# Talking-heads attention and squared-ReLU feed-forward: fifteen fused tiles instead of twenty in the first batch, and a third score block of 64 queries

## The chip, the cores and the metric

The kernel runs on one core of one Trainium2 chip. The metric is the device time of one execution in microseconds (us); lower is better.

The core has a matrix engine (TensorE; PE in the profile, PEld for its weight loads), a vector engine (DVE), a scalar engine (ACT), a general engine (POOL) that here also issues the loads from HBM, and SyncE (SP), whose queue issues the copies between on-chip tensors ("gathers") and the stores of the output. Matrix products land in PSUM, which this program uses as eight banks; operands lie in SBUF.

## The reference

Eight batches, twelve heads, 448 queries and keys, head size 64. What is computed, cut to what matters:

```python
scores = np.matmul(q, k.transpose(0, 1, 3, 2)) / np.sqrt(64)
scores = np.einsum('bhij,hg->bgij', scores, w_pre)      # mix the 12 heads
attn = softmax(scores, axis=-1)
attn = np.einsum('bhij,hg->bgij', attn, w_post)         # mix them again
x = np.matmul(attn, v)                                  # then (b, s, h*d): 3584 rows of 768
h = np.maximum(x @ w_in, 0.0)                           # 768 -> 2048
out = (h * h) @ w_out                                   # 2048 -> 768
```

## The kernel before

**Tiles and steps.** A batch's 448 queries are cut into 45 tiles of ten (the last has eight). A tile holds 12 heads x 10 queries = 120 rows of 448 scores, so that mixing the heads is one matmul with a fixed 120x120 matrix. The program is one list of steps, one tile per step, eight batches one after the other. Step `i` does the head mixing and the exponential of tile `i` (`mix`), and four steps later (`LAG`) the second mixing (`unmix`), whose result DVE copies out of PSUM (L461). Between these, attention-times-V units (`av_unit`), transposes of the next batch's q and k (`turn_unit`) and feed-forward units (`ffn1_unit`, `ffn2_unit`) are put in at fixed steps or as "filler", spread over the steps by weights. Each engine runs its instructions in program order; nothing is chosen at run time.

**Two ways to mix.** In the usual way, `score_burst` computes the scores of a block of 128 queries for six heads at a time (L365; L371 where the block is the short one of 64 queries, in which two heads share a matmul's columns). ACT and DVE copy them from PSUM into a tile `S` (L375, L377). `S` has two buffers, used in turn: a block can be written only when all gathers that read the block two before it have landed. Then `gather` copies the rows of one tile from `S` into a tile `G` of 120 rows with a DMA on SP's queue (L394; where the tile lies in the short block, two DMAs of half the heads, L397; where it lies across the border to it, three), and `mix` is one matmul (L426). `G` has twelve buffers. In the first batch the first `FUSED` tiles are made without scores and gathers: DVE multiplies q by the mixing weights ahead of time (`mix_queries`, L196), and `mix` is six matmuls straight from k and those products (L412).

**Order.** `ORDER` lists the tiles of the first batch by step. In it, gathered tiles stand between fused ones in pairs. `gathered` is the list of all gathered tiles in that order. From step 2 on, each step may issue up to two gathers, up to ten (at the start twelve) ahead of the gathered tiles mixed so far (`AHEAD`). A burst hangs on a gather: `BURSTS[b][blk]` names the gathers of block `blk`, counted from the block's first tile (`FIRST`), behind which the next block's bursts stand in the program. `STARTS` gives each block's first query. `EARLY` says from which steps the first batch's feed-forward units, in thirds of the queries, become filler: (step, third, from, to).

**Loads.** POOL issues the loads of w_in (L266, `W1_AT`), w_out (L272, `W2_AT`), v (L249, L253) and the next batches' q and k (L88, `KQ_AT`) at fixed steps. SP's DMAs go round eight completion semaphores, and the ninth in a row waits for the first to land.

## Time and profile before

| | |
|---|---|
| time, median of 3 runs | 591.75 us (590.99 to 591.92) |
| the profiled execution | 590.49 us, its span 588.7 us |
| granted TensorE clock | 0.999 |
| busy share | PE 96%, PEld 62%, DVE 68%, ACT 65%, POOL 60% |
| DMA | 72.28 MB, mean 123 GB/s |
| HBM | read 47.28 MB, written 11.01 MB |
| SP's queue (gathers and stores) | 36.1% of 16 engines' span |
| POOL's queue (loads) | 30.8% of 16 engines' span |

The busy share of PE is that of modelled matmul ends, which overlap the next matmul's start; start to start tells more than the duration of one. All times of the trace are counted from the span's start. "Idle before <-X" names what ended the idle time of an engine.

### The profile page before, as it was taken

Reading aid. Unit: us, or ns where it says so; the run is one execution under the profiler, and the core shown is the slowest. Engines: PE = TensorE matmul, PEld = TensorE weight load, DVE = VectorE, ACT = ScalarE, POOL = GpSimd, SP = SyncE. Lnnn points to the kernel's source line nnn. Section 1 sums busy time; section 2 is a strip of 40 time slices with the busy share of each in tenths; the row PEclk is TensorE's granted clock in tenths of the full one; section 3 lists DMA queues with packets and bytes.
Section 4 is the critical chain, followed back from the end, with each engine's and each line's share of the span. In section 5 each row is a group of like instructions: output and inputs, shape, how many; then the busy total and the mean of one; then the engine's idle time right before and its main releaser. Section 6 shows DMA issues by size and latency. Waiting matters only on the chain.

```text
span 588.7 us, 18500 instructions
## 1 busy us (share of the span) xinstructions
PE 566.1 (96%) x6735; PEld 363.0 (62%) x6735; DVE 401.1 (68%) x995; ACT 380.3 (65%) x1114; POOL 355.2 (60%) x812
## 2 busy tenths in 40 slices
PE   3999999998999999999999999999999999999996
PEld 2577767665566565666665665665565666666554
DVE  7766759777777667866877578867777667755011
ACT  3756878576886558775876558775677648862410
POOL 6576895465677338783578437783387436772730
PEclk9999999999999999999999999999999999999999
DMA  9999999599568754697558955687544865432113
GB/s 128 146 192 188 182 199 179 109 140 193 118 116 144 162 120 90 115 152 150 109 97 132 166 119 100 118 148 149 107 75 70 131 135 106 87 49 55 28 27 82
DMA packets 85579, 72.28 MB, mean 123 GB/s; under 512 B 18768, under 2 KB 80496, under 8 KB 85488
## 3 DMA queue, kind: packets, MB, share of 16 engines
q1 hardware_dynamic: 49354, 47.30, 36.1%
q0 software_dynamic: 35552, 23.60, 30.8%
q8 instruction: 53, 0.87, 0.6%
q14 instruction: 38, 0.31, 0.2%
q10 hardware_dynamic: 582, 0.21, 0.2%
HBM read 47.28 MB, written 11.01 MB: 99 GB/s over the span
## 4 chain that ended last, share of the span: by engine, by line
PE 82%; DMA 9%; ACT 4%; DVE 2%; POOL 1%; issue 1%; SPq 0%; ACTq 0%; POOLq 0%
PE o_ps L323 24%; PE h_ps L279 23%; PE m_ps L426 10%; PE at_ps L455 9%; DMA G<-S 7%; PE ot_ps L228 5%; PE s_ps L365 4%; ACT S L375 2%; ACT e L430 2%; PE m_ps L412 2%; PE tr_ps L213 2%; PE ot_ps L235 2%; PE at_ps L459 1%; DMA kst<-in_k_dram 1%; PE s_ps L371 1%
## 5 line engine op out<-in xcount | busy, mean ns | idle before, releaser
L430 ACT ACTIVATE e<-m_ps 120x448 bf16<-120x448 f32 x360 | 196.2, 551 | 85.2 <-PE m_ps L426 47.5
L461 DVE CAST at<-at_ps 128x480 bf16<-128x480 f32 (+1 forms) x360 | 206.4, 591 | 62.9 <-PE at_ps L459 46.8
L440 POOL TENSOR_SCALAR pn<-post,rc 120x120 bf16<-120x120 bf16 (+1 forms) x340 | 122.6, 371 | 169.1 <-DVE rc L437 101.8
L279 PE MATMUL h_ps<-xt,w 128*128 128x448 bf16 (+2 forms) x960 | 169.3, 315 | 0.4 <-DVE at L461 0.2
L323 PE MATMUL o_ps<-w,h 128*128 128x384 bf16 x768 | 138.7, 326 | 0.4 <-ACT e L430 0.2
L426 PE MATMUL m_ps<-G,pre 120*120 120x448 bf16 (+1 forms) x340 | 121.3, 357 | 3.5 <-ACT S L375 1.4
L279 PEld LDWEIGHTS <-w 128*128 128x128 bf16 x960 | 84.0, 97 | 56.9 <-issue 6.9
L455 PE MATMUL at_ps<-pn,e 120*128 120x120 bf16 x1080 | 115.9, 216 | 3.1 <-ACT S L375 2.1
L290 POOL TENSOR_TENSOR h<-hr 128x384 bf16<-128x384 f32 (+1 forms) x144 | 105.7, 736 | 21.6 <-ACT hr L285 19.9
L455 PEld LDWEIGHTS <-e 120*128 120x128 bf16 x1080 | 85.5, 98 | 49.3 <-ACT S L375 5.4
L285 ACT ACTIVATE hr<-h_ps 128x448 f32<-128x448 f32 (+2 forms) x160 | 76.2, 480 | 50.0 <-PE h_ps L279 37.0
L323 PEld LDWEIGHTS <-h 128*128 128x128 bf16 x768 | 73.1, 98 | 47.9 <-issue 4.7
L375 ACT CAST S<-s_ps 128x448 bf16<-128x448 f32 x177 | 82.4, 552 | 13.7 <-PE s_ps L365 10.2
L377 DVE CAST S<-s_ps 128x448 bf16<-128x448 f32 x141 | 79.7, 612 | 2.8 <-DMA G<-S 2.4
L430 ACT ACTIVATION_READ_ACCUMULATOR e<-m_ps 120x1 f32 x360 | 75.7, 210 | 0.0
L332 DVE COPY osb<-o_ps 128x384 f32<-128x384 f32 x54 | 30.0, 556 | 57.0 <-PE o_ps L323 56.8
L437 DVE RECIPROCAL rc<-sm 120x2 f32<-120x2 f32 (+1 forms) x192 | 31.1, 162 | 47.9 <-ACT e L430 34.2
L426 PEld LDWEIGHTS <-pre 120*120 120x120 bf16 (+1 forms) x340 | 44.9, 132 | 19.0 <-issue 10.8
L443 POOL TENSOR_TENSOR en<-e,rc 120x128 bf16<-120x128 bf16 (+1 forms) x112 | 42.5, 380 | 0.0
L241 ACT CAST xt<-ot_ps 128x450 bf16<-128x450 f32 (+1 forms) x48 | 25.4, 532 | 25.7 <-PE ot_ps L235 25.2
L365 PE MATMUL s_ps<-kT,qT 64*128 64x448 bf16 x276 | 40.5, 357 | 1.6 <-ACT e L430 0.7
L228 PE MATMUL ot_ps<-at,v 128*64 128x150 bf16 x864 | 41.5, 229 | 0.0
(62 smaller groups left out, 473.4 us busy)
## 6 DMA issues: line engine op xcount, KB each, us to landing
G<-S SPq DMA_DIRECT2D x276, 105.0 KB
out_dram<-osb SPq DMA_DIRECT2D x54, 192.0 KB
kst<-in_k_dram POOLq DMA_DIRECT2D x14, 336.0 KB, 6.3
qst<-in_q_dram POOLq DMA_DIRECT2D x14, 336.0 KB, 6.1
G<-S SPq DMA_DIRECT2D x70, 52.5 KB
v<-in_v_dram POOLq DMA_DIRECT2D x8, 384.0 KB, 8.1
w<-in_moe_w_in_dram POOLq DMA_DIRECT2D x6, 512.0 KB, 11.0
w<-in_moe_w_out_dram POOLq DMA_DIRECT2D x8, 384.0 KB, 8.0
```

The costliest lines, as they stand in the source:

```text
L228: nc.tensor.matmul(ps[64 * hh:64 * hh + 64, TQ * y:TQ * y + TQ], lhsT=vts[b % 2][:, g, r, :], rhs=at[:, r, g, :, :].rearrange("p t i -> p ...
L279: nc.tensor.matmul(ps[:, 0:n], lhsT=w1[ft // 8][:, c2, ft % 8 * 128:ft % 8 * 128 + 128], rhs=xts[b][:, c2, n0:n1], start=(c2 == 0), stop=( ...
L285: nc.scalar.activation(out=hr[:, 0:n], in_=ps[:, 0:n], func=ACT.Relu)
L290: eng.tensor_tensor(out=dst[:, x - o:y - o], in0=hr[:, x - n0:y - n0], in1=hr[:, x - n0:y - n0], op=ALU.mult)
L323: nc.tensor.matmul(ps[:, 0:384], lhsT=lhsT, rhs=w2[ft // 4][:, ft % 4, nt * 384:(nt + 1) * 384], start=(ft == 0), stop=(ft == FT - 1))
L375: nc.scalar.copy(out=sb[:, h, :], in_=ps[:, 0:S])
L377: nc.vector.tensor_copy(out=sb[:, h, :], in_=ps[:, 0:S])
L426: nc.tensor.matmul(ps[0:n, 0:S], lhsT=m[0:n, 0:n], rhs=Gs.pop(s)[0:n, :], start=True, stop=True)
L430: nc.scalar.activation(out=e[0:n, x, :], in_=ps[0:n, 0:S], func=ACT.Exp, scale=SCALE, accum_out=sm[0:n, x:x + 1])
L440: nc.gpsimd.tensor_scalar(out=esb[(b, t - z)][1][0:rows, :], in0=(post_gi if fused else post)[0:rows, :], scalar1=rc[0:rows, z:z + 1], sca ...
L455: nc.tensor.matmul(ps[:, RG * r:RG * r + RG], lhsT=e[0:n, tl % 2, P * r:P * r + P], rhs=pn[0:n, :], start=True, stop=True)
L461: nc.vector.tensor_copy(out=ats[(b, third)][:, 0:k, :, tl, :], in_=ps[:, 0:k * RG].rearrange("p (r g i) -> p r g i", r=k, i=IQ))
```

## The change

In the first batch only fifteen tiles (0 to 14) are fused; tiles 15 to 44 are gathered. The order of the steps is new: after the seven fused tiles at the start comes one gathered tile, then fused and gathered tiles take turns in pairs up to step 21, and from step 22 on all tiles are gathered, in order. The scores of the first batch are cut into three blocks that start at queries 150, 256 and 384, in place of two that start at 200 and 320; the last has 64 queries, as in the other batches. So block 0 serves tiles 15 to 25, block 1 tiles 26 to 38, block 2 the rest of tile 38 and tiles 39 to 44. The bursts hang on other gathers: those of block 1 on the tiles at 4 and 8 of block 0, that of block 2 on tile 6 of block 1 (tile 32), those of the next batch's block 0 on tiles 2 and 4 of block 2 (tiles 41 and 43; before, tiles 40 and 43). The filler of the first thirds of the feed-forward begins at steps 29, 34 and 39 (before 26, 32, 38).

```diff
-FUSED = 20
+FUSED = 15
-ORDER = [0, *range(1, 7), 20, 21, *range(7, 11), 22, 23, *range(11, 15), 24, 25, 15, 16, 17, 26, 27, 18, 19, *range(28, 45)]
+ORDER = [*range(7), 15, 7, 8, 16, 17, 9, 10, 18, 19, 11, 12, 20, 21, 13, 14, *range(22, 45)]
-STARTS = {0: (FQ, S - 128)}
-FIRST = {0: (FUSED, 32)}
-BURSTS = {0: ([4, 8], [8, 11])}
+STARTS = {0: (FQ, 256, 384)}
+FIRST = {0: (FUSED, 26, 39)}
+BURSTS = {0: ([4, 8], [6], [2, 4])}
-EARLY = ((26, 0, 0, 2), (32, 0, 2, 4), (38, 1, 0, 4), (52, 2, 0, 4))
+EARLY = ((29, 0, 0, 2), (34, 0, 2, 4), (39, 1, 0, 4), (52, 2, 0, 4))
```

In `score_burst` and `gather` the short block is known by its start (a query past 320) and no longer by its number 3. In `mix` the first batch takes its mixing matrix as the others do, so that the tiles of the short block get the one with the halved order of heads:

```diff
+        short = q0 > S - P
-                if blk < 3:
+                if not short:
-            for c in range(2 if blk == 3 else 0):
+            for c in range(2 if short else 0):
...
-            if blk < 3:
+            if STARTS[b][blk] <= S - P:
...
-            m = pres[max(x for x in pres if x <= t)] if b else pre
+            m = pres[max(x for x in pres if x <= t)]
```

## The prediction

> **What bounds the kernel now.** I read the chain of waits first, in order of time, over the whole span:

> ```profile
> 14.43 2.51 PE m_ps L412 x6
> 17.60 1.28 PE m_ps L412 x6
> ...
> 23.53 10.45 DMA G<-S
> 34.64 1.14 PE m_ps L412 x6
> ...
> 41.02 14.22 DMA G<-S
> ```

> Columns: start, length, what. A warm fused tile costs PE 1.14 us, six matmuls of 0.19. From 34 us on PE follows itself, one fused tile behind another, and PE is busy 9.95 of 10 us between 30 and 40 us (busy time by stretches), while DVE has 5.5. The start of the program is PE's. But two gathers stand in the chain: the fourth, issued at 23.53, lands at 33.98; the eighteenth, issued at 41.02, lands at 55.24, after 14 us. So fourteen gathers land in 21.26 us, **1.52 us each**, however early they are issued. The DMA view of 40 to 66 us tells why:

> ```profile
> q0 software_dynamic: 2877, 3.23, 79.6%
> q1 hardware_dynamic: 1878, 1.55, 21.9%
> ```

> POOL's loads and SP's gathers fill all sixteen engines (79.6 + 21.9). Between 23 and 60 us the gathers come as fast as the loads let them.

> Third, the timeline of batch 1's end, where one burst's eviction meets a late gather:

> ```profile
> 131.67 0.99 PE L365 MATMUL s_ps<-kT,qT 64*128 64x448 bf16 x6
> ...
> 132.59 0.40 PE L426 MATMUL m_ps<-G,pre 120*120 120x448 bf16 x1
> ...
> 134.47 1.84 ACT L375 CAST S<-s_ps 128x448 bf16<-128x448 f32 x4 [2.21 <-DMA G<-S]
> 134.53 1.16 DVE L377 CAST S<-s_ps 128x448 bf16<-128x448 f32 x2 [2.02 <-DMA G<-S]
> 135.05 0.17 PEld L455 LDWEIGHTS <-e 120*128 120x128 bf16 x3 [2.34 <-ACT S L375]
> 135.05 0.33 PE L455 MATMUL at_ps<-pn,e 120*128 120x120 bf16 x3 [2.07 <-ACT S L375]
> ```

> The block for these scores takes the `S` buffer that tile 44's gather still reads. That gather lands at 134.21 (completion counts of SP's queue). Until then ACT and DVE stand, in order, with everything behind them; PE does one more mixing, has six of eight banks full of scores, and stops until 135.05, **0.84 us after the landing**. In the first batch of before this wait costs nothing: the next batch's burst (step 30) takes the buffer of tiles 20 to 31, the first twelve gathers, landed by 43.2.

> **The change, part by part.**

> *Fused tiles.* Five times six L412 matmuls become five L426: 5 x (1.14 - 0.19) = 4.7 us less on PE, all before step 28, where PE bounds. DVE loses five eighths of six L196 operations (0.65 us each, about 2.1 us, not on the path at 5.5 to 6.6 of 10).

> *Third block.* Twelve L371 matmuls on quarters of the array and six evictions, four on ACT (0.55) and two on DVE (0.61), at step 22. Its buffer is that of the first eleven gathers, the last of which landed at 41.7 in before; step 22 falls at about 42. Should ACT hold PE up there, the time comes out of the stall of step 31, below, so I put it at nothing; without that cover it is ACT's 2.2 us.

> *Pairs.* The third gather (landed 32.20) is wanted at step 11, about 30.6, and PE waits 1.6 us; the others up to step 21 are there. Five gathers more, and eight more DMAs, since tile 38 takes three and 39 to 44 two each: 0.77 us each on SP, and the eight semaphores now hold about four tiles. SP has idle time; it costs only if the gathers become the bound.

> *They do, at the burst of (1, block 0).* It hangs on tile 41, gather 27 of the new list. That is issued in the program when seventeen gathered tiles are mixed, which is step 31. The blocks now take buffers 0, 1, 0, 1, so this burst waits for block 1's readers, tiles 26 to 38: the first DMA of tile 38 is the 24th gather. Behind the waiting evictions stand, on ACT, the exponentials from step 32 and the ReLUs, on DVE the L461 copies and reciprocals, and behind these PE's banks, POOL, and the w_out loads from step 32 on.

> When does the 24th land? At 1.52 us each from the eighteenth: 55.24 + 6 x 1.52 = 64.4. Before's own 24th (tile 43) landed at 64.57 by the completion counts, next in line as soon as the one before it was through, so an earlier issue gains little. Nearer bound: v's small packets pass between 55 and 59 us and gathers 19 to 22 landed 0.8 us apart there (57.10 to 59.53); if SP's earlier issue and the w_out loads held back by the stall stretch that, 62.3. I take 64.4, the rate of the whole stretch. PE reaches the burst at 53 to 54 (4.7 us less work, 1.6 us waited, then the sixteenth and seventeenth gathers at 50.4 and 52.8), so all of the gain is waited away. PE goes on at 64.4 + 0.84 = 65.2, after the mixing of step 32. In before that place is here (PE's timeline):

> ```profile
> 59.31 0.35 PE L426 MATMUL m_ps<-G,pre 120*120 120x448 bf16 x1
> 59.50 0.32 PE L455 MATMUL at_ps<-pn,e 120*128 120x120 bf16 x3
> ```

> 65.2 - 59.5 = **5.7 us later**.

> *EARLY.* Before, eight feed-forward units of six L279 matmuls (0.39 us) were done by then. After, they begin behind step 29, whose transposes are charged against them: about three by step 32. Five are left for the steps behind the stall, where PE stands little (0.3 us between 60 and 67): 5 x 0.39 = **1.95 us**. The floor is nothing, if they fill waits for ACT between 67 and 82, where PE, start to start, stood 2.5 us in all.

> *After that* the queues are self-timed, and PE is nearly dense from 150 us to the end, so the delay stays. Block (1, 1) has the same wait for tile 44 at step 40: SP can issue that by 67 and it lands by 70 to 72, while step 40 comes at about 75.

> **Sum:** 5.7 + 1.95 = 7.65. On the profiled execution's 590.49 (span 588.7 and 1.8 around it) that is 598.1; the median of the runs, 591.75, lies 1.26 higher, so **599.4 us**.

> *After the stall PE may be cold.* Rows: the first fused tile took 2.51 us, one 3 us later 1.28; the first stood behind a PE that had mostly waited for loads, and the slow spacing ended near 17.2 us. PE would stand for about 10 us here. If it starts slow again as at 14.4 to 17.2, that is up to 1.4 us (1.23 for the tile and a little for two scores); ACT, with 2.2 us of evictions to make good, sets the pace in just that time. I take nothing and put 1.4 into the range. [...]

> **Rivals.**

> 1. *Each tile waits for its own gather only*, the buffer being free in time. From step 28 on the same step needs a gather five places further down. Setting before's landings against before's uses, the shortest margin is that of step 43: it needs the 29th, landed 73.93, and stood at 72.32, so 1.6 us late. With 0 to 1.95 for the filler, 593.4 to 595.3. For it: the margins of steps 28 to 39 are positive (1.6 to 5.6). Against it: the wait on eight semaphores ahead of every burst's evictions is in the trace.
> 2. *Faster: PE's saving comes through.* 4.7 less 1.6 for the third gather is 3.1, so 588.6. The point that decides is the landing of tile 38's first DMA: below about 57 us the burst stands no longer than the gain, below 54 not at all. For it: PE is the bound up to 45 us, and the ACT and DVE shares leave room. Against it: the DMA engines would have to move six more gathers by then beside the same loads.
> 3. *A second wall*: tile 44 lands after step 40 since its DMAs are halves, four tiles to the eight semaphores, with w_out loads beside them; and PE starts cold. 3 to 6 us more, 602.4 to 605.4.
> 4. *No difference*: saving and stall cancel; only by chance.

> **How the numbers follow.** A measurement of this kernel can tell about 0.2%, 1.2 us, from no change. The forecast has 0.72: its own range is 595.4 (landing at 62.3, filler at nothing) to 600.8 (a cold PE's 1.4 on top). Rival 1 has 0.10, rival 2 0.08, rival 3 0.08, no difference 0.02. The range takes in rival 1 and most of the third: 593.4 to 603. Slower by over 0.2%: 0.90; within: 0.02; faster: 0.08.

> **What the changed profile would show.** 90 L412 and 345 L426. In the chain, a DMA G<-S that ends between 62 and 65 us. On ACT, an L375 with idle time <-DMA G<-S of some 8 to 10 us near 64, DVE's L377 likewise, and a hole in PE from about 55 to 65; the slice there drops from 9 to 3 or less. Right behind it, fused or feed-forward groups at twice their length if PE is cold. From 100 us on, the same stages 6 to 9 us later. The prediction is wrong if PE has no hole over 3 us near 60, if tile 38's gather lands before 58, or if the later stages make up the delay.

## The result: 1.6% slower

The changed kernel takes 600.35 us (median of 5 runs, 599.86 to 601.78) against 591.75 before: ratio **1.016, 95% interval 1.014 to 1.018**. Forecast were 599.4 us and a range of 593.4 to 603.0. The profiled execution is 599.86 us, its span 598.0, the mean granted clock 0.989. The changed lines are in the order of before, from L359 on one number higher: L366 and L372 the score matmuls, L376 and L378 the evictions, L395 and L398 the gathers, L427 the gathered mixing, L431 the exponential.

### The profile page after: what moved, and what is told of

Same layout as the page of the kernel before. It is cut to its first block, busy times and chain, and to the rows that moved or that the text cites. A ratio compares the mean times of both kernels' runs of the same rounds, so it can differ in the third digit from the quotient of the medians.

```text
span 598.0 us, 18513 instructions
## 1 busy us (share of the span) xinstructions
PE 568.5 (95%) x6722; PEld 363.7 (61%) x6722; DVE 401.9 (67%) x997; ACT 383.3 (64%) x1118; POOL 356.6 (60%) x812
## 4 chain that ended last, share of the span: by engine, by line
PE 84%; ACT 5%; DMA 5%; issue 2%; POOL 2%; SPq 1%; DVE 1%; ACTq 0%; POOLq 0%
PE o_ps L323 24%; PE h_ps L279 23%; PE m_ps L427 11%; PE at_ps L456 9%; PE ot_ps L228 5%; PE s_ps L366 4%; DMA G<-S 4%; ACT S L376 2%; ACT e L431 2%; PE ot_ps L235 2%; PE tr_ps L213 2%; PE m_ps L413 2%; PE at_ps L460 2%; PE s_ps L372 1%; DMA kst<-in_k_dram 1%
## 5 line engine op out<-in xcount | busy, mean ns | idle before, releaser
L431 ACT ACTIVATE e<-m_ps 120x448 bf16<-120x448 f32 x360 | 196.3, 551 | 86.6 <-PE m_ps L427 46.9
L441 POOL TENSOR_SCALAR pn<-post,rc 120x120 bf16<-120x120 bf16 x345 | 125.1, 373 | 174.1 <-DVE rc L438 107.8
L279 PE MATMUL h_ps<-xt,w 128*128 128x448 bf16 (+2 forms) x960 | 171.1, 318 | 0.9 <-ACT hr L285 0.9
L427 PE MATMUL m_ps<-G,pre 120*120 120x448 bf16 x345 | 124.1, 360 | 7.4 <-ACT S L376 5.5
L279 PEld LDWEIGHTS <-w 128*128 128x128 bf16 x960 | 85.6, 99 | 63.0 <-issue 13.6
L376 ACT CAST S<-s_ps 128x448 bf16<-128x448 f32 x181 | 84.3, 552 | 19.3 <-PE s_ps L366 10.4
L378 DVE CAST S<-s_ps 128x448 bf16<-128x448 f32 x143 | 81.3, 615 | 8.7 <-DMA G<-S 7.0
L431 ACT ACTIVATION_READ_ACCUMULATOR e<-m_ps 120x1 f32 x360 | 75.7, 210 | 0.0
L438 DVE RECIPROCAL rc<-sm 120x1 f32<-120x1 f32 (+1 forms) x192 | 31.2, 162 | 46.0 <-ACT e L431 30.9
L427 PEld LDWEIGHTS <-pre 120*120 120x120 bf16 x345 | 45.9, 133 | 20.7 <-issue 11.5
L366 PE MATMUL s_ps<-kT,qT 64*128 64x448 bf16 x276 | 41.0, 367 | 1.8 <-ACT e L431 1.0
```

Source lines behind the costliest of these rows:

```text
L279: nc.tensor.matmul(ps[:, 0:n], lhsT=w1[ft // 8][:, c2, ft % 8 * 128:ft % 8 * 128 + 128], rhs=xts[b][:, c2, n0:n1], start=(c2 == 0), stop=( ...
L376: nc.scalar.copy(out=sb[:, h, :], in_=ps[:, 0:S])
L378: nc.vector.tensor_copy(out=sb[:, h, :], in_=ps[:, 0:S])
L427: nc.tensor.matmul(ps[0:n, 0:S], lhsT=m[0:n, 0:n], rhs=Gs.pop(s)[0:n, :], start=True, stop=True)
L431: nc.scalar.activation(out=e[0:n, x, :], in_=ps[0:n, 0:S], func=ACT.Exp, scale=SCALE, accum_out=sm[0:n, x:x + 1])
L441: nc.gpsimd.tensor_scalar(out=esb[(b, t - z)][1][0:rows, :], in0=(post_gi if fused else post)[0:rows, :], scalar1=rc[0:rows, z:z + 1], sca ...
```

## The profile after

The slices of the page (each a fortieth, 15 us):

```profile
PE   4997799998999999999999999999999999999996
PEclk9998799998999999999999999999999999999999
DMA  9999699669657965688647965688643865432113
```

PE falls to 7 in the fourth and fifth slice (45 to 75 us), and the granted clock to 8 in the fourth and 7 in the fifth. A smaller dip of both stands in the tenth (135 to 150 us). Before, the clock was 1.00 in every stretch, from 17.3 us on, where the trace's records of it begin. The chain of waits, in order of time (start, length, what), is to be read against that of before:

```profile
24.81 10.57 DMA G<-S
...
36.03 1.14 PE m_ps L413 x6
...
41.59 1.19 DMA G<-S
...
43.64 0.95 ACT S L376 x2
44.60 0.43 ACT S L376
45.03 1.59 ACT e L431 x6
...
51.91 2.17 issue
...
58.75 3.82 DMA G<-S
62.76 0.54 ACT S L376
63.34 0.53 PE m_ps L427
```

Four new things. The **fifth** gather (24.81 to 35.38) sets the pace at 35 us. The evictions of the **third block** and the exponentials behind them are in the chain from 43.6 to 46.6. At 51.9 PE stands 2.17 us for no wait that the profile shows. And a DMA G<-S ends at 62.57: the **wall** that was forecast at 62 to 65. The DMA view of 40 to 66 us, packets, MB and share of sixteen engines per queue:

```profile
q0 software_dynamic: 2581, 2.82, 67.6%
q1 hardware_dynamic: 2160, 1.76, 26.9%
```

SP's gathers move 1.76 MB where they moved 1.55, POOL's loads 2.82 where they moved 3.23: the stalled POOL issues fewer. The timeline at the wall (start, busy, engine, line, what, idle before and its releaser):

```profile
57.05 1.30 PE L366 MATMUL s_ps<-kT,qT 64*128 64x448 bf16 x6
...
58.28 0.75 PE L279 MATMUL h_ps<-xt,w 128*128 128x150 bf16 x6
...
62.76 1.84 ACT L376 CAST S<-s_ps 128x448 bf16<-128x448 f32 x4 [5.70 <-DMA G<-S]
62.83 1.16 DVE L378 CAST S<-s_ps 128x448 bf16<-128x448 f32 x2 [5.01 <-DMA G<-S]
63.34 0.53 PE L427 MATMUL m_ps<-G,pre 120*120 120x448 bf16 x1 [4.30 <-ACT S L376]
...
63.66 0.96 PE L279 MATMUL h_ps<-xt,w 128*128 128x150 bf16 x6
```

It is the picture that the prediction drew from batch 1's end: PE has its scores done at 58.4, ACT and DVE stand 5.7 and 5.0 us for a gather, and PE goes on 0.6 us behind the first evictions. Before, the same mixing (step 32) began at 59.31, so PE leaves the wall **4.0 us later** than before. Behind it the matmuls take nearly twice their time: from start to start, six L279 of 150 columns take 0.75 us here and 0.39 in before (by the chains of waits; the groups last 0.96 and 0.55 us).

The windows of the trace show how that goes with the clock (stretch, length, PE, PEld, DVE, ACT and POOL busy with their instructions, granted clock, DMA share, GB/s); the stretches are laid between the places where the granted clock changes:

```profile
51.80:55.20 3.40, 1.23 (x40) 0.99 (x34) 2.05 (x8) 0.25 (x3) 1.78 (x4) 1.00 1.03 188
55.30:58.60 3.30, 3.30 (x24) 1.94 (x22) 1.88 (x5) 1.56 (x6) 1.20 (x3) 0.50 1.12 203
58.80:62.10 3.30, 0.23 (x4) 0.14 (x2) 0.00 (x0) 0.00 (x0) 0.00 (x0) 1.00 0.72 146
62.30:65.50 3.20, 2.16 (x17) 1.94 (x17) 1.70 (x4) 2.75 (x8) 0.63 (x2) 0.50 0.52 116
65.50:68.90 3.40, 3.40 (x25) 2.25 (x23) 1.29 (x4) 1.96 (x8) 2.89 (x7) 0.50 0.75 103
69.10:72.40 3.30, 3.30 (x72) 2.90 (x72) 2.25 (x6) 3.30 (x13) 1.77 (x4) 1.00 0.50 113
```

The clock changes at 55.3, 58.7, 62.1 and 69.0, steps of 3.4 us and once two of them. In these six stretches the clock goes with how busy PE was in the stretch *before*: 1.23 us busy, then 0.50; 3.30 busy, then 1.00; 0.23, then 0.50; 2.16, still 0.50; 3.40, then 1.00. So PE works at half clock from 63.34 to 68.95, **5.6 us**, and ahead of the wall from 55.3 to 58.7, where the wall covers it.

Where the delay arises is seen by counting steps. The table gives the start of the exponential of a step, minus that of before, from one profiled execution each, in us (a negative number is earlier than before); the last column is the span's difference. The other rows are the experiments below. The profiled execution of own block was 2.3 us faster than the median of its runs, that of own block with light loads 1.9 us, so their last columns come out lower than the ratios given below.

| kernel | step 28 | 31 | 32 | 39 | 45 | 105 | end |
|---|---|---|---|---|---|---|---|
| the change | -3.65 | -2.12 | +4.88 | +9.52 | +8.79 | +9.78 | +9.27 |
| own block | -4.82 | -5.48 | -4.33 | -0.44 | +0.51 | +2.29 | +1.85 |
| blocks alone | +0.12 | -1.62 | +0.92 | +0.46 | +0.70 | +2.47 | +1.9 |
| filler first | -4.59 | -1.70 | +4.86 | +7.04 | +6.31 | +5.36 | +5.9 |
| early alone | -0.24 | -2.05 | -2.43 | +1.18 | +0.45 | +0.37 | -0.4 |
| warm (14) | -3.96 | -4.49 | +3.69 | +8.26 | +7.53 | +8.50 | +8.5 |
| warm longer (30) | -4.78 | -5.45 | +4.61 | +8.28 | +7.55 | +9.26 | +9.7 |
| loads later | -4.46 | -4.84 | +2.22 | +6.53 | +5.80 | +4.82 | +5.1 |
| own block, light loads | -4.66 | -4.31 | -3.17 | +0.39 | -0.36 | -0.92 | -0.8 |
| combined | -4.26 | -1.39 | -0.59 | +1.23 | +0.50 | +5.50 | +5.2 |

## The experiments

The theory: the gain of the shorter fused part is real up to step 28, is waited away where burst (1, block 0) waits for tile 38's gather, and that wall with what stands behind it (the filler, a cold PE) makes the loss. The rivals: each tile waits for its own gather in any case; the third block costs the time; the moved filler does.

### Own block: the wall alone taken away

```diff
-            Sb[(b, blk)] = work.tile([P, H, S], BF16, name="S", tag="S", bufs=2)
+            if (b, blk) == (0, 2):
+                Sb[(b, blk)] = late[2].rearrange("p (h s) -> p h s", s=S)
+            else:
+                Sb[(b, blk)] = work.tile([P, H, S], BF16, name="S", tag="S", bufs=2)
```

> The changed kernel, but the scores of the first batch's short block (0, 2) go into memory of their own (the late buffer of the mixed queries, free after the last fused tile) instead of the S buffer, so that the burst of (1, block 0) at step 31 takes the buffer of tiles 15 to 25 and no longer waits for tile 38's gather. Theory (the buffer wait at step 31 is what costs): ACT's idle time before L376/L377 <-DMA G<-S near 60 us is gone, PE has no hole over 3 us there, and the time falls to 590 to 595 us, 593 likeliest, with the tiles' own gathers the next bound. Rival (late gathers as such, or the extra evictions, cost): the hole only moves to the tiles' own gathers and the time stays at 597 us or more.

Measured: 594.6 us (592.34 to 596.98), ratio 1.0069 [1.0042, 1.0097]. ACT's evictions of burst (1, block 0) begin at 53.54 without idle time, the clock is 1.00 from 45 to 90 us, and at step 32 the kernel is 4.33 us *ahead* of before (2.4 of it is filler put off, as early alone shows). So the buffer's wait made the wall, and the wall with what stands behind it more than half of the loss (1.58% against 0.69%). But the lead of steps 28 to 38 is gone at step 45. What PE waits for between 50 and 78 us (us in total, times, longest):

```profile
PE m_ps L430 <- DMA G<-xt: 2.7, 3, 1.3
PE m_ps L430 <- ACT hr L285: 0.6, 1, 0.6
```

L430 is this kernel's gathered mixing, and `xt` the memory of its third block. By the completion counts the gathers of tiles 38 to 42 land at 63.92, 66.03, 68.15, 70.28 and 72.38, **2.1 us apart**, two half DMAs each (tile 38 has a third), and every one of them is used within 0.13 to 0.40 us. The first rival is the next wall. Then follows a third one at 90 us, on ACT:

```profile
90.44 1.84 ACT L379 CAST S<-s_ps 128x448 bf16<-128x448 f32 x4 [2.08 <-DMA G<-S]
```

PE stands 2.0 us there and its clock is 0.89 in the 15 us behind.

### Blocks alone: twenty fused tiles, three blocks

```diff
-STARTS = {0: (FQ, S - 128)}
-FIRST = {0: (FUSED, 32)}
-BURSTS = {0: ([4, 8], [8, 11])}
+STARTS = {0: (FQ, 256, 384)}
+FIRST = {0: (FUSED, 26, 39)}
+BURSTS = {0: ([3, 5], [11], [2, 4])}
```

with before's `ORDER` and `EARLY`, and the lines that know the short block by its start.

> The kernel before with its twenty fused tiles, its order and its EARLY, but with the three score blocks (from 200, 256 and 384) and the bursts of (1, block 0) on tiles 41 and 43, so with the same buffer wait at step 31; tile 38 is now the 19th gather and not the 24th. Theory (the price is the wait for tile 38, set by how many gathers stand before it): the 19th landed at 57.1 us in the kernel before, which reached step 31 at 57.7; wait under 1 us, time 591.5 to 593.5. Rival (the third block, its evictions and the split gathers cost by themselves): 596 us or more.

Measured: 593.07 us (590.42 to 595.41), ratio 1.0044 [1.0025, 1.0063]. The blocks cost 0.4% without one fused tile fewer. The wait that the theory had put at under 1 us isn't there at all: tile 38's first DMA, the one that reads the shared buffer, landed at 56.92, and the burst's evictions on ACT begin at 58.79, behind a ReLU that had waited 1.1 us for POOL. Step 32 is 0.92 us late, step 39 0.46. The rest comes between steps 85 and 90: PE stands 2.5 us at 133.6 (2.1 in before, at 133.0), and the clock is half from 135.6 to 139.0.

### Filler first: eight units ahead of the wall

```diff
-EARLY = ((29, 0, 0, 2), (34, 0, 2, 4), (39, 1, 0, 4), (52, 2, 0, 4))
+EARLY = ((29, 0, 0, 2), (31, 0, 0, 0), (34, 0, 2, 4), (39, 1, 0, 4), (52, 2, 0, 4))
```

> The changed kernel, with the first eight feed-forward units pressed into step 30 and just behind it, so that about seven of them and not three are done before the burst that waits. Theory (the filler that EARLY moved behind the stall is paid in full): 4 x 0.39 = 1.6 us less, 598.8. Rival (they fill waits for ACT behind the stall anyway): within 0.5 us of 600.35.

Measured: 596.4 us (595.44 to 598.78), ratio 1.0108 [1.0083, 1.0134]. The wall is where it was (step 32: +4.86 against +4.88), but at step 45 the kernel is 2.5 us less late, and the tenth slice's dip of the clock is gone, so that at step 105 it is 4.4 us less late (5.36 against 9.78). Together that is more than the 1.6 us expected: the filler itself gives 2.5, the rest comes from the tenth slice. The units put ahead of the wall did not move it: step 32 is late by the same 4.9 us.

### Early alone: before with the moved filler

```diff
-EARLY = ((26, 0, 0, 2), (32, 0, 2, 4), (38, 1, 0, 4), (52, 2, 0, 4))
+EARLY = ((29, 0, 0, 2), (34, 0, 2, 4), (39, 1, 0, 4), (52, 2, 0, 4))
```

> The kernel before with the changed EARLY alone (filler from steps 29, 34 and 39 in place of 26, 32 and 38). Theory (the moved filler costs only because the wait of step 31 stands ahead of it): without that wait the filler's 8 units of 0.39 us are done a few steps later beside the same work, so within 0.6 us of the kernel before, ratio 0.999 to 1.001. Rival (the later start of the filler costs its own time, since PE is dense behind step 34): 1 to 2 us, ratio 1.0017 to 1.0034.

Measured: 589.57 us (588.5 to 590.61, 12 runs) beside 590.3 for before, ratio 0.9983 [0.9971, 0.9996]. The filler left out is worth 2.05 us at step 31, is paid between steps 38 and 39 (from -1.41 to +1.18), and the sum is nothing or a little less (the theory had 0.999 to 1.001). So the moved filler costs only where a wall stands between the saving and the paying: the wall eats the 2.05, the paying stays.

### Warm: PE kept busy in front of the wall

```diff
+        if (b, blk) == (1, 0) and 0 in pairs:
+            for _ in range(14):
+                nc.tensor.matmul(ps[:, 0:S], lhsT=qTs[b][rs, p, q0:q0 + P], rhs=kTs[b][rs, p, :],
+                                 start=True, stop=True)
```

The second kernel has 30 in place of 14.

> The changed kernel, with the last score matmul of the first burst of (1, block 0) repeated fourteen times into the same bank, so that PE has work while the evictions wait. Theory (a cold clock adds to the stall): the granted clock between 60 and 75 us rises from 0.77 to 0.9 or more, the matmuls behind the stall take 0.35 to 0.55 us and not 0.5 to 0.96, and the time falls by 1 to 2.5 us, to about 598.5. Rival (ACT's backlog sets the pace behind the stall, as the prediction took it): the clock rises, the time stays within 0.5 us of 600.35.

> The changed kernel in which the last score matmul ahead of the wait of step 31 is repeated 30 times (some 5.8 us at 0.19 us each) so that PE stands for under 2 us instead of 5; the values are unchanged. With 14 repetitions PE still stood 3.6 us, and its granted clock was 0.5 from 61 to 67 us. Theory (the stall costs more than its length since PE works at half its clock for some 6 us behind it): the granted clock stays at 1.0 behind the wait, the exponential of step 45, 8.8 us late in the changed kernel and 7.5 with 14 repetitions, is 5.5 to 7 us late, and the ratio is 1.009 to 1.012. Rival (the loss behind the wait is the queue of filler and evictions, which ACT and DVE set): the clock is 1.0 but step 45 stays 7.5 to 8.8 us late, ratio 1.014 or more.

Measured: 598.68 us (ratio 1.0145 [1.012, 1.017]) and 598.66 (1.0133 [1.0109, 1.0157]). With 14 the clock is still half from 60.8 to 67.6, since PE stands from 58.2 to 62.1; between 60 and 75 us it is 0.77, as in the change. So the time fell by what that theory forecast, 1.7 us, but not for its reason: tile 38's first DMA landed at 61.27 and not at 62.46, and PE left the wall 1.2 us sooner. With 30, PE stands only from 60.4 to 63.1, and yet:

```profile
57.20:60.60 3.40, 3.23 (x21) 1.62 (x20) 0.00 (x0) 0.00 (x0) 0.00 (x0) 1.00 0.73 147
60.70:64.00 3.30, 0.93 (x13) 0.83 (x13) 1.16 (x2) 1.51 (x4) 0.00 (x0) 1.00 0.54 126
64.20:67.50 3.30, 3.30 (x26) 2.24 (x23) 1.72 (x5) 2.14 (x10) 2.85 (x7) 0.52 0.61 72
67.70:71.00 3.30, 3.30 (x66) 2.82 (x66) 2.11 (x6) 3.30 (x12) 1.76 (x5) 1.00 0.73 152
```

Behind the stretch with 0.93 us of work the clock of the next was 0.52. The cold time behind the wall fell from 5.6 us to 3.4, not to nothing, so the test does not do all that it was made for: step 45 came 7.55 late, at the lower end of the rival's 7.5 to 8.8 and outside the theory's 5.5 to 7. What it does give is a price, if the count starts where PE leaves the wall. From its mixing of step 32 to that of step 45 PE loses 4.8 us against before in the change (4.03 to 8.82 late), 4.7 with 14 repetitions (2.84 to 7.56), whose cold time is 5.5 us, and 3.8 with 30 (3.76 to 7.58). So 2.2 us of half clock less gave 1.0 us back, somewhat under half. For 5.6 us that is an estimate of 2.5 us, and 2.8 us if matmuls take twice their time throughout; no run isolates it.

### Loads later: fewer loads beside the late gathers

```diff
-W2_AT = (28, 30, 32, 34, 36, 39, 42, 45)
+W2_AT = (32, 33, 34, 35, 36, 39, 42, 45)
```

> The changed kernel with the w_out loads of steps 28 and 30 issued at steps 32 to 35 instead, that is behind the wait of step 31; the computation is unchanged. Theory (the 24th gather lands late because the gathers share the DMA engines with the loads): tile 38's DMAs, landed at 64.72 in the changed kernel, land 0.5 to 1.5 us sooner, PE's first mixing behind the wait moves from 63.34 to 62 to 63, and the end from 9 us to 7.5 to 8.5 us behind the kernel before: ratio 1.0125 to 1.0145. Rival (SP's order and its eight semaphores set the landing, not the loads): landing and end move by less than 0.3 us.

Measured: 596.03 us (595.69 to 601.71), ratio 1.0108 [1.0076, 1.014]. The timeline at the wall:

```profile
60.09 1.84 ACT L376 CAST S<-s_ps 128x448 bf16<-128x448 f32 x4 [5.93 <-DMA G<-S]
60.17 1.15 DVE L378 CAST S<-s_ps 128x448 bf16<-128x448 f32 x2 [5.25 <-DMA G<-S]
60.68 0.53 PE L427 MATMUL m_ps<-G,pre 120*120 120x448 bf16 x1 [5.60 <-ACT S L376]
```

Two loads of 384 KB moved behind the wall bring it 2.7 us forward, and tile 38's last DMA from 64.72 to 60.24: more than expected, and in the direction of the theory. That SP's order alone sets the landing falls. The wall is as long as in the change, though, since PE came to it sooner (at step 31 the kernel is 4.84 us ahead of before, the change 2.12).

### Combined, and its loads put into before

The combined kernel is own block, filler first and the loads at (36, 38, 40, 42, 44, 46, 48, 50); the other is before with these loads alone.

> The changed kernel with block (0, 2) in memory of its own, with the filler's first units let in from step 31, and with the eight w_out loads issued at steps 36 to 50. Theory (what is left behind the removed wait, 4.2 us in the run with its own block, is gathers 25 to 30 late by 1.3 to 1.5 us each at steps 34 to 39, then the second burst's wait at 88 to 90 us): fewer loads beside these gathers bring them in time, so up to 3 us of 4.2 come back and some of the cut of 4.7 us may show: 587.5 to 592.5, ratio 0.995 to 1.002. Rival (the waits only move to the steps at which the w_out loads now fall, and to the feed-forward's second product, which needs them): no better than the run with its own block, ratio 1.006 to 1.009.

> The kernel before with the w_out loads alone moved, to steps 36 to 50 as in the combined kernel: what that edit is worth without the change. Theory (in the kernel before nothing on the path waits for gathers between 55 and 75 us, and the loads are wanted only from step 60 on): within 0.8 us, ratio 0.9985 to 1.0015. Rival (gathers beside the later loads land late, or the burst at 134 us waits longer): slower by 1 to 3 us.

Measured: 596.21 us, ratio 1.0085 [1.0063, 1.0108], and 594.32, ratio 1.0052 [1.0033, 1.007]. The rivals were right in both (the second, by its ratio, with 3.1 us just over its 1 to 3). At step 45 the two stand at +0.50 and -0.27, and by step 105 at +5.50 and +4.66. In the second kernel 2.6 us of that come by step 54, where ACT's evictions wait 1.6 us for a gather at 90 us; 0.9 by step 70, where PE waits 0.65 us for w_out itself; and 1.4 by step 90, where PE stands 2.5 us ahead of 138.7 and the clock is half from 140.2 to 143.7. The chain of before with later loads (in the chain of before w_out does not stand at all):

```profile
87.54 19.36 DMA w<-in_moe_w_out_dram
...
131.56 6.29 DMA G<-S
```

So the loads can't be moved out of the gathers' way; they meet the next batch's gathers and their own user. Behind step 45 the control loses 4.9 us and the combined kernel 5.0, though not at the same steps (+1.31 at step 60 against +2.40).

### Own block with light loads, and its control

Six of the eight w_out loads are cut to a quarter of their columns, 1.77 MB less; the rest of w_out is left out of the computation.

```diff
+        m = 0 if x > 5 else 576
-        nc.gpsimd.dma_start(out=w2[x // 2][:, c:c + 2, :],
+        nc.gpsimd.dma_start(out=w2[x // 2][:, c:c + 2, m:DMODEL],
```

> The kernel before with six of the eight w_out loads cut to a quarter of their columns (the rest of w_out is left out of the computation; all matmuls are still done): 1.77 MB less for the DMA engines from step 28 on. A control for the next kernel. Both theories: before has no wait for a gather there that costs time, so within 1 us of the kernel before, ratio 0.998 to 1.001.

> The changed kernel with block (0, 2) in memory of its own (no wait at step 31) and the same cut of the w_out loads. Theory (with the wall gone the saving of 4.7 us is eaten by gathers 25 to 30, which come late because the DMA engines are full with them and the loads): with lighter loads they land in time and 2 to 4.7 us of the saving come through against the control, ratio to the kernel before 0.991 to 0.997. Rival (the loss is not the DMA engines' but the moved filler's and ACT's and DVE's evictions): no more than 1 us below the control, ratio 0.998 or more.

Measured: the control 590.37 us (ratio 0.9992 [0.9977, 1.0007]), own block with light loads 591.6 (1.0016 [0.999, 1.0042]; its 12 runs spread from 588.4 to 596.17). The lighter loads are worth nothing to before and about 0.5% to own block (1.0069 to 1.0016, on two chips). The gathers of steps 38 to 42 (out of `xt`), for which own block waited 2.7 us between 50 and 78 us, no longer hold PE up (in that stretch it waits 1.3 us in all for gathers, of `S`), so the DMA engines' load was behind that wall. But the saving of 4.7 us does not come through: theory wrong by its numbers, rival right in its numbers. What PE waits for between 28 and 57 us says where the rest went; own block with light loads:

```profile
PE m_ps L431 <- DMA G<-S: 2.3, 4, 0.8
PE ot_ps L228 <- DVE at L466: 0.8, 1, 0.8
...
```

and the kernel before, in the same stretch, in all:

```profile
PE at_ps L455 <- DVE qT L215: 0.2, 1, 0.2
PE m_ps L426 <- ACT e L430: 0.2, 1, 0.2
```

Counted from matmul start to matmul start, PE stands some 3 to 5 us longer between 10 and 94 us than in the control, by how small a gap is still counted: most of the saving, or all of it. Of these, 1.3 are the fourth and fifth gather at 33 to 34.4; 1.9 at 43.9 to 47.8 are ACT's exponentials and one DVE copy behind the third block's evictions; 1.6 are gathers that land at 53.3 and 55.9. No run takes these three away one by one.

## Why the prediction was right, point by point

*The fused cut* gave about what the rows said: own block is 4.82 us ahead at step 28, of which 0.24 is filler put off, against 4.7 worked out. In the change it is 3.65, with 1.5 already waited for gathers. That all of it is waited away was right.

*The third gather* was the wrong one. Issued at 22.05, 0.4 us sooner than in before, it landed at 27.43 and not at 32.20. The fourth and fifth waited, landing at 34.03 and 35.38, for 0.6 and 1.0 us. Their sum, 1.5 us, is near the forecast's 1.6 by luck, since the place is another.

*The third block at nothing* was right for the change and for the reason given, the cover of the wall. The price without cover, put at ACT's 2.2 us, shows as 1.9 us of waits behind the block's evictions in own block with light loads. In blocks alone, where fewer gathers stand ahead, steps 39 to 85 are 0.5 to 0.7 us late.

*The burst at step 31* was the step that carried the forecast, and it happened: ACT 5.7 and DVE 5.0 us idle on DMA G<-S (forecast 8 to 10), PE's hole from 58.7 to 63.3 (forecast from 55). Two terms in it were too large. The first DMA of tile 38 released the evictions at 62.57, near the lower bound of 62.3 and not at the 64.4 that was taken; gathers 19 to 23 came 0.8 us apart (58.69 to 61.88), as the prediction's nearer bound had it, and it is tile 38's last DMA that landed at 64.72. And PE went on 0.6 to 0.8 us behind that. So 4.0 us in place of 5.7. The holes also differ because PE came later to the burst (57.05, where 53 to 54 was forecast), after the unforeseen 2.2 us at 52 and the half clock behind them.

*EARLY* was put at 1.95 us. Early alone shows 2.05 us saved ahead of the wall and 2.6 paid behind; filler first got 2.5 back. Mechanism and size were right, a little low.

*The cold PE* is the step that failed, as far as the runs show: it was taken as nothing, with 1.4 in the range, because ACT was thought to set the pace just behind the wall. The clock stood at half for 5.6 us of PE's work, not for the 2.8 us of slow spacing that the first fused tiles showed: behind the stretch with 0.23 us of work it was 0.50, and behind the next, with 2.16 us, it stayed there. The price, an estimate of 2.5 us, is above the 1.4. The view of before gives a granted clock of 1.00 ahead of 17 us as well, where its first fused tile took 2.51 us; the trace's records of the clock begin only at 17.28, where the slow spacing ended, so that they say nothing against a cold start.

*The sum* was thus right by errors that cancel: up to step 45 the forecast had 5.7 + 1.95 + 0 = 7.65, measured are 8.79, in which 4.0 are the wall and 2.5 the filler; the 2.3 that are left fit the cold PE (an estimate of 2.5, as above), which is worked out and not isolated. That ACT's backlog has a part in them is not ruled out: ACT's four evictions behind the wall put the exponential of step 32 4.88 us late, where its matmul is 4.03.

*After that the delay stays.* Nearly: it was 8.79 at step 45, 8.45 at 60, 9.78 at 105 after a second stall of PE (1.8 us, to 143.3) with a half clock from 144.0 to 147.5, and 9.27 at the end. Block (1, 1) did not wait for tile 44, as forecast (landing 72.65, used by a step that came at 78). The wall that own block shows at 90 us belongs to another burst.

*The rivals.* The first, each tile's own gather, was given 593.4 to 595.3 if the buffer were free: own block measured 594.6. The second, faster by the saving, fails even in the kernel without wall and with light loads. Of the third, the second wall was not seen in the change, the cold PE was.

No version of the change beat before. Early alone is 0.17% faster [0.04, 0.29], less than the 0.2% set as the bound at the start.

## What to carry to other kernels

Taking work off the engine that is busiest only pays if what replaces it has a free resource: here five tiles moved from PE to DMA engines whose share from 23 to 60 us was 1.05 before and is 1.05 in the change, and every wall removed showed the next one (buffer, own gather, third block's evictions). A change in the number of blocks of a ring of buffers changes *which* readers a later writer waits for; follow the ring by hand before costing the work. And after a stall of 2 to 3 us look at the granted clock in the stretch that follows: behind holes of 2.0, 2.2 and 2.6 us it was half for 3.4 us, longer than the hole, while filler put ahead of the wall in filler first made step 45 2.5 us less late.

## What the runs showed of the hardware that was not expected

The hole at 51.9 follows no wait in the profile. Beside it, at 51.86, an instruction packet of 16,384 bytes passes on queue 8 and takes 0.93 us, while the DMA engines are at a share of 1.03. That PE waited there for its instructions is a guess: between 20 and 160 us 14 such packets pass in the change and 15 in before, and this hole is the only one of that size in PE for which the profile shows no wait. The kernels with other instructions ahead of that place (own block, both warm ones) have no such hole.
